# Turning the rows of eight weight-gradient blocks by DMA ahead of time, and storing them turned

## The chip, the cores and the metric

The kernel runs on one core of a Trainium2 chip. The metric is the device time of one execution in microseconds (us). A core has five engines that run side by side, each with its own queue of instructions in a fixed order: TensorE (PE: matrix products and turns of 128 x 128 blocks), VectorE (DVE), ScalarE (ACT), GpSimd (POOL) and SyncE (SP). SyncE, ScalarE and GpSimd also issue the transfers (DMAs), which run on 16 DMA engines that all queues share. An engine that waits for something holds all that is queued behind it on that engine.

## The reference

It is the backward pass of a gated mix of two branches over a sequence of L = 2048 positions with D = 448 features; all arrays are bf16. Cut to what matters:

```python
# branch A (S4): y = conv(u, K) + u * Dskip, K from A, B, C (D x 256), by FFT of 2L
# branch B: h = x @ w1 + b1; r = max(h, 0); out = (r * r) @ w2 + b2     F = 1792
g = sigmoid((u * gate_w).sum(-1, keepdims=True))
out = g * a(u) + (1 - g) * b(x)
_out, _vjp = jax.vjp(_f, u, A_re, A_im, B_re, B_im, C_re, C_im, log_dt, Dskip, w1, b1, w2, b2, gate_w)
_grads = _vjp(grad_out)            # the mix and 14 gradients are returned
```

The input x of branch B is the same array as u. With dB = (1 - g) * grad_out, the gradient of w2 (F x D) is (r * r)^T @ dB, and that of w1 (D x F) is u^T @ dh, with dh = 2 r * (dB @ w2^T). The change concerns the first of these.

## The kernel before, in words

L is cut into 16 tiles of 128 positions, F into FT = 14 blocks of 128 rows, D into 14 chunks of 32 channels for the S4 branch (NCH = 14, line 30).

The stages, in the order of the code:

- Lines 445 to 619: first transforms of u and of the gated gradient, load and turn of inputs (0 to about 230 us).
- Lines 991 to 1032, the **S4 chunks**, with c from 0 to 14: powers are built on VectorE (`build_x`, `build_y`), their tables are turned and multiplied on TensorE (`back_z`, `back_p`, `kgen`). Every chunk turns four groups g of Y: three of them by a DMA that SyncE issues (`load_yt`, line 912), the fourth (and all four of the first and the last chunk) on TensorE (`turn_yt`). The last chunk is 13, so the last DMA turn is that of chunk 12.
- Lines 597 to 619 and 1056 to 1063, `hidden`: r in four blocks of 512 positions. It is stored as rows of F in the DRAM array `rT_d` (F x L) in pieces of 256 KB; the last piece is stored at 447.6 us.
- Lines 1064 to 1083: w1 and w2 are turned on TensorE (L1071, L1082). The result of the second is the tile `w2Tv` (tag U16), and the tile `hv` (tag D16) then takes the place of w2. Both leave 1024 columns free, 7168 to 8192, which two of the seven slots of the ring `rr` use (line 1086).
- Lines 1100 to 1128 and 1152, `row_block`: dh in four blocks of 512 positions, and its product with w1 (`project`). The pieces of r come back from `rT_d` by ScalarE's queue into the ring `rr`, `NR - 3` steps ahead (L1096); VectorE multiplies (L1122) and GpSimd stores the rows of dh in `dhT_d` (L1123).
- Lines 1130 to 1155: the S4 kernel `k_d` is loaded again in another order (`X<-k_d`, L1139 and L1142, on SyncE) and transformed (L231); the transform's parts are stored and loaded again.
- Lines 1347 to 1361: the **gradient of w2**, `grad_w2(j)` for 14 blocks, then the first two of w1, with the products of the spectra (`product`) and the gradients of A, B, C (`param_grads`) woven in.
- Lines 1374 to 1460: the outputs, the remaining parameter gradients and the remaining 12 blocks of the gradient of w1.

For one block of w2 `gradrows` (line 1173) loads 128 rows of `rT_d` (512 KB) by GpSimd's queue into one of two raw buffers (L1185), turns them on TensorE in two times eight blocks of 128 x 128 into PSUM (L1190), squares them on ScalarE on the way from PSUM into one of two buffers `hn` (L1191), and multiplies them with the 16 tiles of dB (L1196, 16 products of 128 x 448). ScalarE copies the result (L1201) and GpSimd stores it (L1202). The gradient of w1 goes the same way with `dhT_d`; from block JL = 5 on, half of its rows are turned by a DMA of SyncE from DRAM (L1180).

The order on each engine isn't that of the code: a planner with costs and due times of its own orders the queues when the program is built, from what each instruction depends on; instructions earlier in the code have precedence. Work of later stages so fills gaps of earlier ones: in the trace the products of `hidden`, `project` and `row_block` stand between those of the S4 chunks. `tc.issue_after(x)` places instructions behind x on x's engine; it adds no wait. Waits are set where data or memory is needed: a tile whose memory another tile takes over is released by its last reader.

Of the kernel before, what the change touches and what calls it, by code (L numbers as in the profile page):

```python
# [12 lines left out]
ACT = mybir.ActivationFunctionType  # L13
# [6 lines left out]
P = 128  # L20
L, D, N, F = 2048, 448, 256, 1792
LT = L // P
FT = F // P
# [6 lines left out]
NCH = D // CC  # L30
# [308 lines left out]
def kernel(ctx, tc, A_u, A_A_re, A_A_im, A_B_re, A_B_im, A_C_re, A_C_im, A_log_dt, A_Dskip,  # L339
# [3 lines left out]
    nc = tc.nc  # L343
    V, S, G_, T_ = nc.vector, nc.scalar, nc.gpsimd, nc.tensor
# [5 lines left out]
    def dscr(name, n, dt=bf16):  # L350
        return nc.dram_tensor(name, (n,), dt, kind="Internal")
# [12 lines left out]
    rT_d = dscr("rT_d", F * L)  # L364
    dhT_d = dscr("dhT_d", F * L)
    br_d = dscr("br_d", L * 2 * D)

    const = ctx.enter_context(tc.tile_pool(name="const", bufs=1))
    pool = ctx.enter_context(tc.tile_pool(name="mem", bufs=1))
    psum = ctx.enter_context(tc.tile_pool(name="psum", bufs=1, space=PSUM))  # L370
    K = Ker(tc, pool, psum)
# [46 lines left out]
    SB = K.t("S25", [P, 12800])  # L418
# [137 lines left out]
    th, s, q_ = Lr_, dsa[:, 0:2 * D], dsa[:, 2 * D:4 * D]  # L556
# [208 lines left out]
    Ys = [YA[:], KB[:, 6144:14336].rearrange("p (w t b) -> p w t b", t=2, b=64)]  # L765
# [7 lines left out]
    Fv = K.t("F17", [P, 8704])  # L773
# [13 lines left out]
    P2 = K.t("M8", [P, 4096])  # L787
# [34 lines left out]
    def load_rx(c):  # L822
        rx_[c] = K.t("recx", [P, 1024])
        (G_ if c == 1 else nc.sync).dma_start(rx_[c][:], bass.AP(tensor=rec_d, offset=c * P * RS, ap=[[RS, P], [1, 1024]]))
# [87 lines left out]
    def load_yt(c, g):  # L912
        nonlocal yi
        YT = (YTr[yi % 4] if yi % 4 < 3 else P2[:, 2048:4096]).rearrange("p (h i n) -> p h i n", h=2, i=CW)
        yi += 1
        nc.sync.dma_start_transpose(out=YT.rearrange("p h i n -> p (h i) n"), in_=Ys[c % 2][:, 16 * g:16 * g + 16].rearrange("p w t b -> p (w t b)"))
        return YT

    def dk_chunk(c):
# [62 lines left out]
                        G_.dma_start(bass.AP(tensor=(t_d if s else s_d), offset=o_, ap=[[512, 32 * cnt // (1 + s)], [1, 256]]), src)  # L982
        return lastp

    XTs, YTs = {}, {}
    load_rx(0)
    load_ry(0)
    expand_x(0)
# [2 lines left out]
    for c in range(NCH + 1):  # L991
# [15 lines left out]
        for half in range(2):  # L1007
            if c < NCH:
                ay = build_y(c, half, ax if half == 0 else ap or ay)
                if half == 1:  # L1010
                    k_out(c, kgen(c))
                for g in (2 * half, 2 * half + 1):
                    YTs[c].append(turn_yt(c, g, ("S", "N3")) if c == 0 else turn_yt(c, g) if g == 3 or c == NCH - 1 else load_yt(c, g))
                if c + 1 < NCH:
                    if half == 0:
                        lry = load_ry(c + 1)
                        lry1 = lry if c == 0 else lry1
                        expand_x(c + 1)
                        if c == 0:
                            expand_y(1, 0, 4)  # L1020
                    elif c == 0:
                        expand_y(1, 4, 5)
                    else:
                        expand_y(c + 1)
                if half == 0:
                    dk_chunk(c)
            ap = None
            if c > 0:
                ap = back_p(c - 1, XTs[c - 1][half], (z01, z23)[half], (2 * half, 2 * half + 1), ay if c < NCH else None)
# [43 lines left out]
    w2Tv = K.t("U16", [P, 8192])  # L1073
# [9 lines left out]
        S.copy(w2Tw[:, jp], ps[:])  # L1083
    hv = K.t("D16", [P, 8192])
    hblk = hv[:, 0:7168].rearrange("p (j l) -> p j l", j=FT)
    rr = [P2[:, 0:1024], P2[:, 1024:2048], Fv[:, 2048:3072], Fv[:, 3072:4096], SB[:, 8320:9344], w2Tv[:, 7168:8192], hv[:, 7168:8192]]
    NR = len(rr)
    dblk = SB[:, 6272:8320].rearrange("p (a l) -> p a l", a=DT)

# [4 lines left out]
    def load_r(i):  # L1094
        r_ = rr[i % NR].rearrange("p (k l) -> p k l", k=2)
        nc.scalar.dma_start(r_, bass.AP(tensor=rT_d, offset=2 * (i % (FT // 2)) * P * L + 512 * (i // (FT // 2)), ap=[[L, P], [P * L, 2], [1, 512]]))  # L1096
        return r_
    rq = [load_r(i) for i in range(NR - 3)]

    def row_block(lb, banks):  # L1100
        nonlocal ni
# [31 lines left out]
    for (p0, p1) in ((64, 128), (32, 64), (16, 32), (0, 16)):  # L1133
        offs = vp[p0] - LT * p0
        assert all((vp[p] - LT * p == offs).all() for p in range(p0, p1))
        j = 0
# [36 lines left out]
    def gradrows(w, j, nb):  # L1173

        nonlocal hi, ni
        late = w == 1 and j >= JL
        if late:
            raw_, hh = rl[hi % 2], hl[hi % 3]
            with tc.issue_after(lasths.ins):
                nc.sync.dma_start_transpose(out=hh[:, 8:16], in_=bass.AP(tensor=dhT_d, offset=j * P * L + 1024, ap=[[L, P], [1, 1024]]))  # L1180
        else:
            raw_, hh = hr[:, hi % 2], hn[:, hi % 2]
        hi += 1
        nl = L // 2 if late else L
        K.last_raw = G_.dma_start(raw_, bass.AP(tensor=(rT_d if w == 0 else dhT_d), offset=j * P * L, ap=[[L, P], [1, nl]]))  # L1185
        for th in range(1 if late else 2):
            ps = K.ps(nb[ni % len(nb)], [P, 8, P], bf16)
            ni += 1
            for tt in range(8):
                T_.transpose(ps[:, tt, :], raw_[:, (8 * th + tt) * P:(8 * th + tt + 1) * P], ident[:])  # L1190
            S.activation(hh[:, 8 * th:8 * th + 8, :], ps[:], ACT.Square if w == 0 else ACT.Copy)  # L1191
        ps = K.ps(nb[ni % len(nb)], [P, 512])
        ni += 1
        width = D if w == 0 else D + 1
        for t in range(LT):
            lastm = T_.matmul(ps[:, 0:width], lhsT=hh[:, t, :], rhs=(DB2[:, t, :] if w == 0 else U[:, t, 0:D + 1]), start=(t == 0), stop=(t == LT - 1))  # L1196
        return ps, lastm

    def grad_w2(j):
        ps, lastm = gradrows(0, j, NB)  # L1200
        S.copy(dw2s[:, j % 2], ps[:, 0:D])  # L1201
        G_.dma_start(out_12[j * P:(j + 1) * P, :], dw2s[:, j % 2])  # L1202
        return lastm

    def grad_w1(j, nb):
        nonlocal ni
        ps, _ = gradrows(1, j, nb)
        S.copy(dw1r[:, 0:D + 1], ps[:, 0:D + 1])
        S.copy(db1[:, j:j + 1], dw1r[:, D:D + 1])
        ps = K.ps(nb[ni % len(nb)], [P, DT, P], bf16)  # L1210
        ni += 1
        for dt in range(DT):
            z = DSZ[dt]
            T_.transpose(ps[0:z, dt, :], dw1r[:, dt * P:dt * P + z], ident[:])

        j0, nj = (j - j % 2, 2) if j < JS else (JS + (j - JS) // 4 * 4, 4)
        f0, f1, dws = P * j0, P * (j - j0), (dw1a if j < JS else dw1b)
        S.copy(dws[:, 0:3, f1:f1 + P], ps[:, 0:3])
        S.copy(dws[0:64, 3, f1:f1 + P], ps[0:64, 3])
        if j == j0 + nj - 1:  # L1220
            G_.dma_start(bass.AP(tensor=out_10.tensor, offset=out_10.offset + f0, ap=[[F, P], [P * F, 3], [1, P * nj]]), dws[:, 0:3, 0:P * nj])
            G_.dma_start(bass.AP(tensor=out_10.tensor, offset=out_10.offset + 384 * F + f0, ap=[[F, 64], [1, P * nj]]), dws[0:64, 3, 0:P * nj])
# [151 lines left out]
    for q in range(4):  # L1374
# [7 lines left out]
        for x in range(2):  # L1382
            pp = K.pair()
            for hp in range(2):
                t = 2 * q + x + 8 * hp
# [32 lines left out]
    for q in range(4):  # L1418
# [5 lines left out]
        for x in range(2):  # L1424
            ps = K.pair()
            l0l = 2 * q + x
            for hp in range(2):
                t = l0l + 8 * hp
# [62 lines left out]
```

## Time and profile before

Median 921.62 us of three runs, 915.82 to 931.09. The profiled execution has a span of 918.7 us and a mean granted clock of TensorE of 0.846.

| engine | busy us | share of the span |
|---|---|---|
| TensorE, products | 719.5 | 78% |
| VectorE | 657.1 | 72% |
| ScalarE | 591.4 | 64% |
| GpSimd | 201.5 | 22% |
| DMA, hardware queue q1 (SyncE) | 118198 packets, 83.32 MB | 36.7% of 16 engines |
| DMA, software queue q0 (GpSimd) | 21504 packets, 67.46 MB | 22.1% of 16 engines |

| what | from, to (us) |
|---|---|
| S4 chunks' DMA turns, chunk 9 | 475.7 to 483.8 |
| chunk 10 | 519.5 to 529.6 |
| chunk 11 | 551.1 to 559.8 |
| chunk 12 (the last) | 582.1 to 594.8 |
| X<-k_d loads issued | 630.8 to 643.4 |
| third transform's first products (L231) | 649.6 to 662.0 |
| last row block (L1110) | 650.2 to 674.7 |
| DMA engines over 0.95 busy, TensorE mostly idle | 685 to 700 |
| gradient of w2: first turns, last product | 697.8 to 808.0 |
| gradient of w1: first turns, last product | 807.9 to 908.5 |

How to read it: the averages hide that the bound changes. VectorE is nearly full in the S4 chunks, the DMA engines are from 650 to 700 us, TensorE and VectorE in turn after it. A line of the timeline has the start, the length from first start to last end, the engine, the line of the code, the operation, the tiles by their tags (U, D, S, ... are the first letters of the pool's tags; ps with a letter is a bank of PSUM) and the count; in brackets the idle time before it and what ended it. The products' lengths overlap, since the array is pipelined: eight turns that follow each other every 0.056 us show 0.61 us.

### The profile page before, as it was taken

The page shows a single profiled execution, that of the slowest core. Times are in us where ns is not written, and L with a number is a line of the kernel's source. Part 1 is how long each engine was busy: PE and PEld are TensorE (multiplying, and loading weights), DVE is VectorE, ACT ScalarE, POOL GpSimd, SP SyncE. Part 2 cuts the span into 40 slices and gives each one's busy share as a digit, 9 for nine tenths or more (in the row PEclk, how much of TensorE's full clock was granted, in tenths as well). Part 3 has the DMA queues.
Part 4 walks back from the last instruction along what each step waited for, and adds up shares of the span by engine and source line. Part 5 has one row for each costly group of instructions (what it writes and reads, how often), then busy time and mean ns, then how long its engine had stood idle before and what let it go on. Part 6 is the DMA issues. An engine that isn't in the chain of part 4 may idle for free. (4 is left out here: it accounts for less than half of the span.)

```text
span 918.7 us, 18982 instructions
## 1 busy us (share of the span) xinstructions
PE 719.5 (78%) x7633; PEld 346.0 (38%) x7633; DVE 657.1 (72%) x1146; ACT 591.4 (64%) x939; POOL 201.5 (22%) x349
## 2 busy tenths in 40 slices
PE   1776755647988988798789887898886888988895
PEld 0332222225344443453356253344332334543352
DVE  4585867697399999979995799993424898859200
ACT  2797768716987868868676777375533765654543
POOL 2241010012202112021122031123231313354220
PEclk9977566667959798899975899899996999998998
DMA  8697675896526665357573567827999999799761
GB/s 229 191 315 254 245 291 218 322 311 188 144 58 123 149 142 115 88 127 155 124 153 79 110 210 164 185 79 202 279 388 293 334 276 350 216 256 279 193 166 52
DMA packets 167295, 184.97 MB, mean 201 GB/s; under 512 B 95187, under 2 KB 144248, under 8 KB 166408
## 3 DMA queue, kind: packets, MB, share of 16 engines
q1 hardware_dynamic: 118198, 83.32, 36.7%
q0 software_dynamic: 21504, 67.46, 22.1%
q10 hardware_dynamic: 27506, 33.00, 11.2%
q8 instruction: 59, 0.97, 0.5%
q14 instruction: 28, 0.23, 0.1%
HBM read 89.60 MB, written 73.13 MB: 177 GB/s over the span
## 5 line engine op out<-in xcount | busy, mean ns | idle before, releaser
L959 DVE TENSOR_TENSOR P<-R 128x2048 bf16<-128x2048 bf16 x42 | 49.6, 1218 | 33.0 <-ACT R L943 22.1
L943 ACT CAST R<-psF 128x1024 bf16<-128x1024 f32 x56 | 57.5, 1027 | 15.5 <-PE psF L939 15.5
L1196 PEld LDWEIGHTS <-S 128*128 128x128 bf16 x448 | 41.9, 100 | 51.9 <-issue 10.0
L1047 PE MATMUL psN<-D,S 128*128 128x448 bf16 x208 | 55.0, 400 | 4.7 <-ACT S L615 4.7
L1196 PE MATMUL psF<-U,S 128*128 128x448 bf16 x224 | 49.8, 369 | 2.8 <-ACT S L1191 2.6
L608 PE MATMUL psN<-S,U 128*128 128x512 bf16 x132 | 41.6, 434 | 8.3 <-ACT F L613 4.7
L939 PE MATMUL psF<-R,S 64*32 64x256 bf16 (+1 forms) x1344 | 38.5, 302 | 11.5 <-DMA R<-Y 7.0
L1110 PE MATMUL psN<-S,U 128*128 128x512 bf16 x126 | 37.8, 420 | 6.9 <-ACT D L1115 6.9
L209 DVE CAST K<-psN 128x448 bf16<-128x448 f32 x36 | 21.7, 619 | 28.9 <-PE psN L259 26.8
L799 DVE TENSOR_TENSOR X<-X,F 128x512 bf16<-128x512 bf16 (+1 forms) x70 | 37.5, 535 | 5.2 <-ACT F L833 3.3
L1123 POOL DMA_DIRECT2D dhT_d<-D x28 | 20.2, 721 | 92.3 <-DVE D L1122 91.7
L810 DVE TENSOR_TENSOR K<-K,F 128x2048 bf16<-128x2048 bf16 (+3 forms) x42 | 36.3, 865 | 5.0 <-ACT F L838 3.5
L810 DVE TENSOR_TENSOR Y<-Y,F 128x2048 bf16<-128x2048 bf16 (+3 forms) x42 | 36.3, 865 | 1.6
L800 DVE TENSOR_TENSOR F<-X,F 128x512 bf16<-128x512 bf16 (+1 forms) x70 | 37.0, 528 | 0.6 <-ACT F L834 0.2
L811 DVE TENSOR_TENSOR F<-K,F 128x2048 bf16<-128x2048 bf16 (+3 forms) x42 | 35.9, 854 | 2.0 <-ACT F L840 2.0
L813 DVE TENSOR_TENSOR K<-K,F 128x2048 bf16<-128x2048 bf16 (+3 forms) x42 | 36.3, 865 | 1.3
L813 DVE TENSOR_TENSOR Y<-Y,F 128x2048 bf16<-128x2048 bf16 (+3 forms) x42 | 36.3, 864 | 1.3
L909 ACT COPY M<-psX 128x1024 bf16<-128x1024 bf16 x26 | 26.5, 1019 | 15.3 <-PE psX L908 15.3
L939 PEld LDWEIGHTS <-S 64*16 64x16 bf16 (+1 forms) x1792 | 22.6, 91 | 36.0 <-issue 27.1
L811 DVE TENSOR_TENSOR F<-Y,F 128x2048 bf16<-128x2048 bf16 (+3 forms) x42 | 35.9, 855 | 0.1
L1047 PE MATMUL psN<-S,D 128*128 128x448 bf16 x168 | 35.7, 361 | 0.0
L803 DVE TENSOR_TENSOR X<-X,F 128x512 bf16<-128x512 bf16 (+1 forms) x70 | 32.4, 462 | 1.8
(412 smaller groups left out, 1948.1 us busy)
## 6 DMA issues: line engine op xcount, KB each, us to landing
sp<-K ACTq DMA_DIRECT2D x8, 896.0 KB, 4.2
hd<-st ACTq DMA_DIRECT2D x16, 448.0 KB, 5.4
dhT_d<-D POOLq DMA_DIRECT2D x28, 256.0 KB, 5.5
R<-sp SPq DMA_DIRECT2D x8, 896.0 KB, 22.2
S<-rT_d POOLq DMA_DIRECT2D x14, 512.0 KB, 7.0
R<-hd SPq DMA_DIRECT2D x16, 448.0 KB, 7.9
rec_d<-F POOLq DMA_DIRECT2D x2, 1920.0 KB, 9.7
Y<-gd SPq DMA_DIRECT2D x4, 896.0 KB, 9.2
```

The costliest lines, as they stand in the source:

```text
L608: T_.matmul(ps[:], lhsT=w1w[:, dt, j * P:j * P + P], rhs=ub[:, dt], start=(dt == 0), stop=False, skip_group_check=True)
L799: V.tensor_tensor(out=hi4, in0=lo, in1=bcast_dims(pr, [0, (None, n), 1]), op=ALU.mult)
L800: V.tensor_tensor(out=Vv.rearrange("p (x a r) -> p x a r", x=2 * W2, r=2), in0=lo, in1=bcast_dims(pi, [0, (None, n), 1]), op=ALU.mult)
L810: V.tensor_tensor(out=hi, in0=lo, in1=bcast_dims(pr, [0, (None, n // 2), 1]), op=ALU.mult)
L811: V.tensor_tensor(out=Vv.rearrange("p (x a q) -> p x a q", x=rows, q=2), in0=lo, in1=bcast_dims(pi, [0, (None, n // 2), 1]), op=ALU.mult)
L813: return V.tensor_tensor(out=T4[:, :, :, n:2 * n], in0=T4[:, :, :, n:2 * n], in1=V4, op=ALU.add)
L939: T_.matmul(psz[32 * ii:32 * ii + m, t, 256 * s:256 * s + 256], lhsT=DKc[64 * t:64 * t + 64, s, g, 2 * ii:2 * ii + 1 + par].rearrange("p i ...
L943: S.copy(zb[:, :, :, gg].rearrange("p s t n -> p t s n"), psz[:].rearrange("p t (s n) -> p t s n", s=2))
L959: lastp = V.tensor_tensor(out=pr.rearrange("p s t g n -> p s t (g n)"), in0=zv, in1=(xb if r == 0 else rev_dim(xb, 2)), op=ALU.mult)
L1047: lastm = T_.matmul(ps[:, 0:D], lhsT=hblk[j][:, P * tt:P * tt + P], rhs=ws[:, j, :], start=(w == 1 and j == 0), stop=(j == FT - 1))
L1110: T_.matmul(ps[:], lhsT=w2Tw[:, jp, dt, j % 2], rhs=dblk[:, dt], start=(dt == 0), stop=False, skip_group_check=True)
L1196: lastm = T_.matmul(ps[:, 0:width], lhsT=hh[:, t, :], rhs=(DB2[:, t, :] if w == 0 else U[:, t, 0:D + 1]), start=(t == 0), stop=(t == LT - 1))
```

## The change

The rows of r for the last eight blocks of w2's gradient (j from JN = 6 to 13) are no longer turned on TensorE in `gradrows`. Earlier, between the last S4 chunks and after them, SyncE turns them by DMA from `rT_d` into SBUF, 1024 positions (256 KB) at a time, and GpSimd stores what was turned in a new DRAM array `rN_d`. In `gradrows` such a block is then loaded from `rN_d` already turned (still 512 KB, still on GpSimd's queue), and ScalarE squares it from SBUF into `hn`. The turns and their pass through PSUM are left out for these blocks; blocks 0 to 5 and the gradient of w1 stay as they were.

The 16 DMA turns share two slots of 1024 columns, the free ends of `w2Tv` and `hv`, one for each half; turn k + 2 can't start before the store of turn k has read the slot. The ring `rr` gives these two slots up and shrinks from seven to five, so that a piece of r is loaded two steps ahead and not four. `yt_ins[c]` keeps the last DMA turn of chunk c; the turns 0 and 1 are placed behind that of chunk 9, 2 and 3 behind that of chunk 10, 4 and 5 behind that of chunk 11, and the other ten behind that of chunk 12. What it is for: to take turns from TensorE in the stage of w2's gradient.

```diff
+    rN_d = dscr("rN_d", 8 * P * L)
...
-        nc.sync.dma_start_transpose(out=YT.rearrange("p h i n -> p (h i) n"), in_=Ys[c % 2][:, 16 * g:16 * g + 16].rearrange("p w t b -> p (w t b)"))
+        yt_ins[c] = nc.sync.dma_start_transpose(out=YT.rearrange("p h i n -> p (h i) n"), in_=Ys[c % 2][:, 16 * g:16 * g + 16].rearrange("p w t b -> p (w t b)"))
...
-    rr = [P2[:, 0:1024], P2[:, 1024:2048], Fv[:, 2048:3072], Fv[:, 3072:4096], SB[:, 8320:9344], w2Tv[:, 7168:8192], hv[:, 7168:8192]]
+    rr = [P2[:, 0:1024], P2[:, 1024:2048], Fv[:, 2048:3072], Fv[:, 3072:4096], SB[:, 8320:9344]]
...
     rq = [load_r(i) for i in range(NR - 3)]
+    JN = FT - 8
+    slots = [w2Tv[:, 7168:8192], hv[:, 7168:8192]]
+    for k in range(16):
+        j, h = JN + k // 2, k % 2
+        with tc.issue_after(yt_ins[min(9 + k // 2, NCH - 2)].ins):
+            nc.sync.dma_start_transpose(out=slots[h].rearrange("p (t f) -> p t f", f=P), in_=bass.AP(tensor=rT_d, offset=j * P * L + 1024 * h, ap=[[L, P], [1, 1024]]))
+        G_.dma_start(bass.AP(tensor=rN_d, offset=(j - JN) * P * L + 1024 * h, ap=[[L, P], [1, 1024]]), slots[h])
...
-        K.last_raw = G_.dma_start(raw_, bass.AP(tensor=(rT_d if w == 0 else dhT_d), offset=j * P * L, ap=[[L, P], [1, nl]]))
-        for th in range(1 if late else 2):
+        turned = w == 0 and j >= JN
+        K.last_raw = G_.dma_start(raw_, bass.AP(tensor=rN_d, offset=(j - JN) * P * L, ap=[[L, P], [1, L]]) if turned else
+                     bass.AP(tensor=(rT_d if w == 0 else dhT_d), offset=j * P * L, ap=[[L, P], [1, nl]]))
+        if turned:
+            for th in range(2):
+                S.activation(hh[:, 8 * th:8 * th + 8, :].rearrange("p t f -> p (t f)"), raw_[:, 1024 * th:1024 * th + 1024], ACT.Square)
+        for th in range(0 if turned else 1 if late else 2):
```

More of the change, by code (lines that the diff above doesn't have):

```diff
@@ L983, in back_p @@
         return lastp
-    XTs, YTs = {}, {}
+    XTs, YTs, yt_ins = {}, {}, {}
     load_rx(0)
```

## The prediction

> **What bounds the kernel now.** I read the windows by stage first, then the timeline of TensorE in the stage the change touches, then the chain that ended last, then the queue of SyncE. The windows below cut the gradient of w2 for blocks 6 to 13 at its block boundaries (770 to 809 us). Columns: us, then busy us (and instructions) of each engine, granted clock, DMA share, GB/s.
>
> ```profile
> core 0: us, PE busy (x) PEld busy (x) DVE busy (x) ACT busy (x) POOL busy (x), PEclk, DMA share, GB/s
> 779.60:784.40 4.80, 4.56 (x37) 2.55 (x37) 4.73 (x9) 3.24 (x6) 1.63 (x3) 1.00 1.08 236
> 789.30:794.00 4.70, 4.51 (x37) 2.57 (x35) 4.67 (x6) 3.18 (x6) 1.50 (x3) 1.00 0.71 221
> 798.90:804.00 5.10, 5.10 (x39) 2.76 (x38) 1.09 (x4) 3.07 (x5) 1.47 (x4) 1.00 0.81 259
> ...
> sum 39.00, PE 37.22 PEld 20.93 DVE 31.98 ACT 23.32 POOL 14.19; mean PE 4.65 PEld 2.62 DVE 4.00 ACT 2.91 POOL 1.77
> ```
>
> TensorE is busy 37.22 of 39.00 us at full clock; VectorE is full until 800 us and then waits. One block in TensorE's timeline (start, us):
>
> ```profile
> 783.34 0.61 PE L1190 MATMUL psX<-ident,S 128*128 128x128 bf16 x8
> 783.79 0.61 PE L1190 MATMUL psS<-ident,S 128*128 128x128 bf16 x8
> 784.33 0.55 PE L314 MATMUL psN<-P,cb_MI 64*128 64x448 bf16 x3
> 785.13 3.20 PE L1196 MATMUL psF<-U,S 128*128 128x448 bf16 x16 [0.25 <-ACT S L1191]
> ```
>
> The two groups of eight turns take the array 783.34 to 784.33 less the start of the next group, 0.45 us each; then 0.55 us of other work, then a wait of 0.25 us for the square, then 3.05 us of the 16 products (the next turns start at 788.31). From the product of block 6 (770.69) to that of the first w1 block (809.73) are 39.04 us for 8 blocks: **4.88 us a block**. The chain leaves this stage by memory that the last product sets free:
>
> ```profile
> 804.99 3.04 PE psF L1196 x16
> 808.85 0.54 POOL U L1410
> ...
> 810.96 6.71 DMA U<-in_A_C_re_dram
> ```
>
> The U tile (gradient rows) is released by the last product, the A, B, C rows are loaded into it, VectorE starts its third parameter group at 815.48 and then runs without a gap to 858. So a block that ends sooner is worth its time at the end, as long as VectorE's own work (full to 800.05 us) doesn't stand in front.
>
> The place where the added work goes is SyncE's queue:
>
> ```profile
> 582.12 12.66 SPq L916 DMA_TRANSPOSE R<-Y  x3
> 630.81 0.32 SPq L1142 DMA_DIRECT2D X<-k_d  x1
> 631.33 12.10 SPq L1139 DMA_DIRECT2D X<-k_d  x10
> ```
>
> Between 594.8 and 630.8 SyncE only waits for k_d. The X loads behind that wait feed the third transform's products, which start at 649.60 with no wait; the last load is issued by 643.4 and lands 4 to 5 us later, so they have some 1.5 us of slack.
>
> **What the Trainium skill says.** "DMA: Bandwidth & Descriptors", section "Anatomy of one DMA", puts some 2 us of fixed cost on a DMA, mostly the receipt of the last write, and says that a wait happens on the issuing sequencer ahead of dispatch. The trace agrees: nothing here lands under 2 us, and SyncE sits in semaphore waits. "Advanced Engine Details and Errata", section "X-Bar Transpose (TRN2)", calls turning DMAs "as fast as regular DMAs". The trace agrees on latency only: 4.2 us median for the nine turned 256 KB loads of the end, as for the plain ones beside them. On occupancy it does not. From 876 to 900 us SyncE's queue moved 1.57 MB in 33.1% of 16 engines, 5.1 us per MB, GpSimd's 2.23 MB in 28.7%, 3.1 us per MB. The measurement decides.
>
> ```profile
> S<-dhT_d POOLq DMA_DIRECT2D x9, 256.0 KB, 4.2
> S<-dhT_d SPq DMA_TRANSPOSE x9, 4.2
> dhT_d<-D POOLq DMA_DIRECT2D x28, 256.0 KB, 5.5
> rT_d<-M POOLq DMA_DIRECT2D x8, 256.0 KB, 3.8
> ```
>
> **Removed.** 8 blocks x 16 turns leave TensorE: 8 x 2 x 0.45 = 7.2 us. The wait for the square before the product goes too (1.05 us for block 6, about 0.2 for five others, none in two): 2.1 us. Sum **9.3 us at most**, a period of 3.7 us. ScalarE keeps two squares of 1024 columns a block; the SBUF source costs the same (L615, SBUF to SBUF, 1.05 to 1.08 us; L1191 from PSUM 1.02). At 3.1 us of 4.88 it fits into 3.7.
>
> **What takes over.** A raw buffer was free when its turns were done; now it is free when its second square is done. Two buffers: the loads of this stage landed in
>
> ```profile
> DMA to landing us min/median/max: 4.0/5.6/8.1
> ```
>
> plus two squares at 0.92 us, 1.84, plus GpSimd's queue, where the load stands behind the store of the block before (it waited 16.1 us in 7 times there, beside PE; I allow 1 us). 5.6 + 1.84 + 1.0 = 8.4 us for two blocks, 4.2 a block: 0.66 us saved, x 8 = **5.3 us**. With landings of 4.0 it is 3.4, so the 3.7 of TensorE holds and 9.3 are saved; with 8.1 it is 5.5, no saving. I take 5.3.
>
> **Added, early.** Turns 0 to 5 follow the last S4 turns of chunks 9, 10, 11. Slot 0 lies in the tile that L1071 frees at 484.6, slot 1 in the one that L1082 frees at 504.5. If turn 1 stood ahead of the recx load of 493.25, that load would land at 504.5 + 1.2 + 0.3 + 3.2 = 509.2 instead of before the expansion at 506.2: 3.0 us on ScalarE, for which VectorE already waits 5.77 us there. On ScalarE the last L1083 copy (505.33) stands just ahead of that expansion, so the planner had the load issued before L1082 was done; I take 0, and keep 3.0. Turns 2 to 5 hold the next recx loads by two issues of 1.24 us; these are issued some 8 us ahead of their expansion (559.9 against 568): 0.
>
> **Added, late.** Ten turns follow the last S4 turn of chunk 12, ending at 594.8. Each slot's cycle is a turn (4.2), a store on GpSimd (0.71 to issue, 3.8 to 5.5 to land, I take 4.5): 9.4 us per pair. Turns 14 and 15 wait for four cycles: 594.8 + 37.6 = 632.4, and take 2.5 us to issue: 634.9. If the k_d loads stand behind all ten they start 4.1 us late, less 1.5 of slack: 2.6 us; ahead of the last pair, 0. Taken: **1.5 us**. Low end of the cycle, 3.4 + 0.7 + 3.0 = 7.1: nothing. High end: a store queued on GpSimd behind a dhT_d store, which waited up to 12.2 us for VectorE.
>
> DMA engines: ten turns x 0.262 MB x 5.1 = 13.3 us and ten stores x 0.262 x 3.1 = 8.1 us, 21.4 in all. The 5 us windows from 595 to 635 have shares of 0.61, 0.35, 0.07, 0.30, 0.25, 0.65, 0.66, 0.58, which leaves 22.6 us free: it just fits, hidden beside the last chunks' matmuls. What runs over 640 meets a share of 0.84 to 1.0 and would cost its own time.
>
> **Edits at nothing.** The ring of r shrinks from 7 to 5 slots. In the last row block step 5's load then waits for step 0's product (664.7) and lands by 669.4 to 672, ahead of its use at 674.3: hidden by the 1.8 us steps between. GpSimd gets 16 x 0.72 = 11.5 us more at 22% busy. DB2's load at 676 waits for slot 0's last store, which lands around 645.
>
> **Sum:** 921.6 - 5.3 + 1.5 = 917.8, **918 us**.
>
> **The rivals.**
> 1. The turns hold SyncE. Stores land late because GpSimd is held by dhT_d stores, so pairs take 12 us: turn 15 is issued at 594.8 + 48 + 2.5 = 645.3, the X loads start 14.5 late, 13 past the slack: 921.6 + 13 - 5.3 = 929. For it: the 12.2 us wait and one queue in order. Against: only four dhT_d stores stand from 605 to 622, and the planner may let the loads overtake. 25%.
> 2. The same, with every store behind such a wait (17 us a pair): 594.8 + 68 + 2.5 = 665, 34.5 late, 33 past the slack, 921.6 + 33 - 5.3 = 949: slower than before. 10%.
> 3. TensorE's full 9.3 us come, nothing is late: 912. For it: landings of 4.0 to 4.7 after 785 us, where DMA share falls to 0.27. Against: VectorE, full to 800. 15%.
> 4. The ring of two raw buffers becomes the bound at 8.1 us landings, no gain: 921.6 + 1.5 = 923. For it: 7.2, 7.8 and 8.1 us for three of seven loads. 8%.
>
> **How the numbers follow.** The forecast has 42%. Its parts alone (landings 4.0 to 8.1, cost 0 to 3) span 912 to 924. Rival 1 reaches from 920 to 935. A range of **909 to 933** leaves out rival 2, part of rival 1's tail and a few per cent below. The three times of before lie from 915.8 to 931.1, so some of the range is that. Faster than 903.2 would need twice 9.3 us: 4%. Slower than 940.1 is rival 2 and a remainder: 11%. Within: 85%.
>
> **What would show it.** Right: a period of about 4.2 us in blocks 6 to 13, L1410 loads some 4 us sooner against the start of the stage, X<-k_d issued by 635, SyncE's turns done before. Wrong: X<-k_d issued after 640 (rivals 1, 2); waits of the square for the raw load of over 2 us a block (rival 4); waits of S4 products for turned tiles grown past today's 12.6 us; or VectorE as the releaser of the products, so that the shorter blocks buy nothing.

## The result, and the profile after

The changed kernel takes **946.63 us** (median of six runs, 942.30 to 955.99); the kernel before took 924.08 us beside it (six runs, 915.82 to 935.40). The ratio is **1.029, 95% interval 1.021 to 1.037**: slower. Medians are over all executions of a kernel, while a ratio and its interval compare only the fast ones of either kernel (within 1.5% of its fastest), so the two can differ. In the later comparisons the median of before was 924.7 to 926.7 us, so 921.6 was a somewhat kind start, and its profiled execution of 918.7 us kinder still. A second profile of the kernel before is used below where that matters (span 914.1 us, called "before, again").

The same stage as in the prediction, the gradient of w2 from the product of block 6 to the first of w1, now lies at 790.5 to 827.9 us. The windows of the changed kernel by stage, three of eight blocks (columns as in the prediction):

```profile
core 0: us, PE busy (x) PEld busy (x) DVE busy (x) ACT busy (x) POOL busy (x), PEclk, DMA share, GB/s
...
799.10:808.80 9.70, 3.20 (x16) 1.48 (x16) 9.60 (x17) 2.89 (x6) 2.17 (x4) 0.88 1.01 282
...
814.00:817.00 3.00, 3.00 (x18) 1.57 (x16) 2.83 (x8) 2.44 (x3) 1.19 (x3) 1.00 0.62 187
...
sum 37.50, PE 28.47 PEld 13.86 DVE 30.05 ACT 19.41 POOL 14.41; mean PE 3.56 PEld 1.73 DVE 3.76 ACT 2.43 POOL 1.80
```

TensorE's busy time in the stage fell from 37.22 to 28.47 us, but the stage only from 39.0 to 37.5. Some 5.7 of these 8.75 us are not saved but moved: 33 products of the inverse transforms (L314, L331, L333) stood between the turns of these blocks and took 6.28 us; in the changed kernel 3 are left (0.55 us), and nearly all of the others run after the stage. The undisturbed block at 814 runs in 3.0 us; the one at 799 takes 9.7, with the DMA engines full. TensorE's timeline says what it waits for (start and length in us; in brackets the idle time before and what ended it):

```profile
794.21 3.20 PE L1209 MATMUL psS<-U,S 128*128 128x448 bf16 x16 [0.54 <-ACT S L1198]
799.19 3.20 PE L1209 MATMUL psF<-U,S 128*128 128x448 bf16 x16 [1.78 <-ACT S L1198]
808.90 5.32 PE L1209 MATMUL psX<-U,S 128*128 128x448 bf16 x16 [6.51 <-ACT S L1198]
814.05 3.19 PE L1209 MATMUL psS<-U,S 128*128 128x448 bf16 x16
```

The squares (L1198) in turn wait for the raw rows. The first line below is from that line's own view (who kept ScalarE idle, us and times), the second from the page's DMA issues (512 KB each, median 6.3 us to landing):

```profile
  DMA S<-rN_d: 14.7, 5
...
S<-rN_d POOLq DMA_DIRECT2D x8, 512.0 KB, 6.3
```

So the gradient gave little. The loss is earlier. SyncE's queue in the changed kernel:

```profile
582.46 11.61 SPq L917 DMA_TRANSPOSE R<-Y  x3
594.16 3.05 SPq L1105 DMA_TRANSPOSE U<-rT_d  x1
...
631.66 1.28 SPq L1105 DMA_TRANSPOSE D<-rT_d  x1
642.95 0.33 SPq L1150 DMA_DIRECT2D X<-k_d  x1
643.38 12.75 SPq L1147 DMA_DIRECT2D X<-k_d  x10
```

The issue of the last turn ends at 632.9 us, 2.0 us *sooner* than I had worked out (634.9). Yet the first load of k_d comes at 642.95, against 630.81 before. SyncE did not hold it: between 633 and 643 it waits for k_d itself. GpSimd's queue has the reason:

```profile
629.32 0.54 POOL L1106 DMA_DIRECT2D rN_d<-D  x1 [5.65 <-DMA D<-rT_d]
...
638.44 0.56 POOL L1106 DMA_DIRECT2D rN_d<-D  x1 [5.38 <-DMA D<-rT_d]
639.00 2.42 POOL L885 DMA_DIRECT2D k_d<-R  x4
```

Four of the last chunk's k_d stores stand behind the store of turn 15. Their data was there at 623; they are issued from 639.0 on. In the kernel before the same four were issued as soon as their data was there:

```profile
624.62 2.43 POOL L884 DMA_DIRECT2D k_d<-R  x4
```

ScalarE issues the other four. Its queue before, and then in the changed kernel:

```profile
625.35 2.65 ACTq L884 DMA_DIRECT2D k_d<-R  x4
628.04 1.01 ACT L909 COPY R<-psX 128x1024 bf16<-128x1024 bf16 x1 [4.44 <-PE psX L908]
```

```profile
623.66 8.25 ACTq L885 DMA_DIRECT2D k_d<-R  x4
631.95 1.01 ACT L910 COPY R<-psX 128x1024 bf16<-128x1024 bf16 x1 [8.79 <-issue]
```

The same four issues took 2.65 us before and 8.25 us beside the turns, and the copies behind them, which the last S4 chunk's products wait for, came 3.9 us later. So there are two suspects for k_d, the **order on GpSimd** and the **slow issue on ScalarE**, and a third, the sheer traffic.

To compare kernels whose executions drift, I count from one event in each: the start of the last product of the S4 kernel (`kgen`, 623.1 us before, 622.6 after).

| us after the last k product | before | before, again | changed |
|---|---|---|---|
| first load X<-k_d | 7.7 | 7.4 | 20.3 |
| first turns of w2's gradient | 74.7 | 75.0 | 88.0 |
| from there to the first product of w1's gradient | 111.9 | 119.7 | 117.3 |
| from there to the end of the span | 109.0 | 109.2 | 112.6 |

13 us are lost at k_d and carried unchanged to the gradient. The third row needs its second column: in blocks 0 to 5 TensorE met a wait of 7 us that the first profile of before did not have. It ends in the evacuations of L208. Before, again:

```profile
754.34 0.53 PE L331 MATMUL psN<-R,negI 128*128 128x448 bf16 x1 [7.04 <-ACT st L208]
```

In the changed kernel it is 7.98 us at 778. It comes and goes without the change, so it isn't counted to it.

### The profile page after: what moved, and what is told of

Read it like the earlier page. It is cut to its first block, busy times and chain, and to the rows that moved or that the text cites. A ratio compares the mean times of both kernels' runs of the same rounds, so it can differ in the third digit from the quotient of the medians.

```text
span 940.5 us, 18791 instructions
## 1 busy us (share of the span) xinstructions
PE 717.7 (76%) x7505; PEld 340.0 (36%) x7505; DVE 656.6 (70%) x1146; ACT 591.7 (63%) x939; POOL 210.6 (22%) x365
## 3 DMA queue, kind: packets, MB, share of 16 engines
q1 hardware_dynamic: 135094, 87.51, 39.6%
## 5 line engine op out<-in xcount | busy, mean ns | idle before, releaser
L800 DVE TENSOR_TENSOR X<-X,F 128x512 bf16<-128x512 bf16 (+1 forms) x70 | 37.4, 535 | 5.2 <-ACT F L834 3.3
L1048 PE MATMUL psN<-S,D 128*128 128x448 bf16 x168 | 38.1, 379 | 2.0 <-DVE D L1130 2.0
L940 PEld LDWEIGHTS <-S 64*16 64x16 bf16 (+1 forms) x1792 | 22.9, 91 | 39.6 <-issue 30.5
L314 PE MATMUL psN<-P,cb_MI 64*128 64x448 bf16 x128 | 29.0, 402 | 9.5 <-ACT st L208 8.2
L1209 PE MATMUL psF<-U,S 128*128 128x448 bf16 x128 | 32.7, 396 | 2.6 <-ACT S L1198 1.8
```

Of the source, the lines that this page charges most:

```text
L800: V.tensor_tensor(out=hi4, in0=lo, in1=bcast_dims(pr, [0, (None, n), 1]), op=ALU.mult)
L940: T_.matmul(psz[32 * ii:32 * ii + m, t, 256 * s:256 * s + 256], lhsT=DKc[64 * t:64 * t + 64, s, g, 2 * ii:2 * ii + 1 + par].rearrange("p i ...
L1048: lastm = T_.matmul(ps[:, 0:D], lhsT=hblk[j][:, P * tt:P * tt + P], rhs=ws[:, j, :], start=(w == 1 and j == 0), stop=(j == FT - 1))
```

## The experiments

Times are medians; "before" is the kernel before in the same comparison, and a ratio has its 95% interval. The edits are against the changed kernel unless "before" is said.

### 1. Which part: the turns, or their use?

Two halves. First, all turns and stores made and the ring cut, but the gradient as it was:

```diff
-        turned = w == 0 and j >= JN
+        turned = False
```

> The changed kernel with all 16 DMA turns and their stores, and the ring of five slots, but the last eight blocks of w2's gradient are loaded from rT_d and turned on TensorE as before. Theory K (the last chunk's k_d stores stand behind the store of the last turn on GpSimd, so the third transform starts 12 us late and that carries to the end): before + 10 to 13 us, a ratio of 1.011 to 1.014 to before, X<-k_d issued at about 643. Rival G (the loss is made in the gradient of w2, where ScalarE waits 14.7 us for turned rows; the 12 us are absorbed while the DMA engines are full): before + 0 to 3 us, ratio 1.000 to 1.003.

Measured: 947.69 us (before 926.26), ratio 1.022 (1.013 to 1.032). X<-k_d 15.2 us after the last k product, first turns of w2's gradient 85.1 after it. So nearly all of the loss is here, and it is larger than I had expected.

Second, the kernel before with the gradient's edit alone, on rows that were not turned:

```diff
# against before
+        turned = w == 0 and j >= JN
+        K.last_raw = G_.dma_start(raw_, bass.AP(tensor=rT_d, offset=j * P * L, ...) if turned else ...
+        if turned:
+            for th in range(2):
+                S.activation(hh[...], raw_[:, 1024 * th:1024 * th + 1024], ACT.Square)
```

> No turns and no stores of them, seven slots in the ring of r as before; the last eight blocks are loaded from rT_d as they are and squared straight from SBUF, without any turn (so these blocks of w2's gradient are of rows that were not turned: the work of turning is left out). Theory K: before - 1 to - 6 us, ratio 0.993 to 0.999. Rival G: before + 6 to 10 us, ratio 1.007 to 1.011, with ScalarE waiting over 10 us for the loads.

Measured: 922.78 us (before 926.26), ratio 0.997 (0.994 to 1.000). So the use is worth some 3.5 us by the medians and 2.4 by the ratio, whose interval just reaches 1: a gain, but less than the 5.3 that I took. Together the halves give 17.9 of the 22.6 us; the first half's interval is wide enough for the rest. The squares waited as they do in the changed kernel; from the view of their line:

```profile
  DMA S<-rT_d: 14.2, 4
```

### 2. How many turns does it take?

Three blocks: the six early turns alone, with the short ring.

```diff
-    JN = FT - 8
+    JN = FT - 3
-    for k in range(16):
+    for k in range(6):
```

> The changed kernel for the last three blocks only: the six early turns (behind chunks 9, 10 and 11), none behind chunk 12. Theory K: nothing stands before the k_d stores; before + 0 to - 2 us (three blocks at 0.66), ratio 0.998 to 1.000. Rival G: three eighths of its loss, before + 2 to + 4, ratio 1.002 to 1.004.

Then five, six and seven blocks, by the same two numbers (`FT - 5` and `range(10)`, `FT - 6` and `range(12)`, `FT - 7` and `range(14)`).

> The changed kernel with five turned blocks in place of eight: ten turns, of which four are late and over by about 612, ahead of the k_d stores at 622. Theory Q: X<-k_d at 624 to 632 as in the kernel before, ratio 0.994 to 1.003. Rival C (each late turn costs its share of the traffic, 4 of 10 late turns): ratio 1.008 to 1.013, and X<-k_d 4 to 5 us late.

> The changed kernel with six turned blocks: twelve turns, six of them late, the last issued at about 615 and its store landed by about 621, just ahead of the k_d stores. Theory T (the cost is a cliff: it starts when turns and their stores reach into the k_d stores and loads, from 622 on): X<-k_d 7 to 10 us after the last k product, as before, ratio 0.998 to 1.005. Rival L (each late turn costs its share, 20 us over the last six): ratio 1.006 to 1.010.

> The same with seven turned blocks: fourteen turns, the last issued at about 623, its store at about 628 ahead of GpSimd's four k_d stores. Theory T: half of the cliff, X<-k_d 12 to 16 us after the last k product (before: 8, changed kernel: 20), first turns of the second weights' gradient 79 to 84 us after it (before: 75, changed kernel: 88), ratio 1.006 to 1.016. Rival (only the last pair of turns hurts, since it alone holds SyncE): ratio 0.998 to 1.005.

| turned blocks | turns after chunk 12 | against before, us | ratio | X<-k_d, us after last k product | first turns of w2, us after it |
|---|---|---|---|---|---|
| 3 | 0 | +0.4 | 1.003 (1.000 to 1.006) | 7.8 | 77.6 |
| 5 | 4 | +1.2 | 1.002 (0.998 to 1.006) | 6.6 | 74.1 |
| 6 | 6 | +3.2 | 1.005 (1.001 to 1.009) | 8.8 | 78.2 |
| 7 | 8 | +17.9 | 1.018 (1.011 to 1.024) | 17.1 | 87.5 |
| 8 | 10 | +22.6 | 1.029 (1.021 to 1.037) | 20.3 | 88.0 |

It is a step, not a slope. Theory T holds in kind and was too mild for seven blocks, where nearly all of the delay is there already (the profile with seven blocks is of the slowest of four executions, 954.9 us). SyncE's queue with six and with seven blocks shows the step:

```profile
613.51 1.28 SPq L1105 DMA_TRANSPOSE D<-rT_d  x1
627.90 0.33 SPq L1150 DMA_DIRECT2D X<-k_d  x1
```

```profile
627.41 1.23 SPq L1105 DMA_TRANSPOSE U<-rT_d  x1
635.29 1.23 SPq L1105 DMA_TRANSPOSE D<-rT_d  x1
647.01 0.33 SPq L1150 DMA_DIRECT2D X<-k_d  x1
```

With six, the last turn is issued 5.6 us ahead of the last k product (619.1) and its store issued at 618.0. With seven, the last one stands 5.4 us behind that product (629.9), and ScalarE's four k_d issues take 9.30 us there instead of 4.74. Even 4.74 is more than the 2.65 of before, though with six blocks every turn had landed by 618.0, ahead of these issues; so a turn under way isn't all that slows them. The early six turns show no cost beyond the noise (the interval reaches 1.006), as I had said.

### 3. Which queue, then?

If GpSimd's order was to blame, ScalarE could issue all eight k_d stores of the last chunk:

```diff
-                    (nc.scalar if jt and c > 9 else G_).dma_start(bass.AP(tensor=k_d, ...
+                    (nc.scalar if c > 9 else G_).dma_start(bass.AP(tensor=k_d, ...
```

> The changed kernel with one edit: the four k_d stores of the last chunk that GpSimd issues behind the last turn's store are issued by ScalarE, right behind the copy that they store. The order of TensorE, VectorE and SyncE stays as it is in the changed kernel. Theory K: X<-k_d is issued at 633 instead of 643 (then held only by SyncE's own last turn), and the time falls by 8 to 10 us against the changed kernel: 936 to 938, ratio to before 1.013 to 1.015. Rival G: the loads are earlier but the time stays within 2 us of the changed kernel, ratio 1.027 to 1.031.

Measured: 941.26 us (before 926.26), ratio 1.021 (1.013 to 1.029); X<-k_d 16.7 us after the last k product, and w2's gradient 87.2 after it. A miss: the wait only changed its queue. ScalarE's queue in this kernel:

```profile
622.84 15.98 ACTq L885 DMA_DIRECT2D k_d<-R  x8
638.86 1.01 ACT L910 COPY R<-psX 128x1024 bf16<-128x1024 bf16 x1 [16.53 <-DMA k_d<-R]
```

Eight issues at 2.0 us each, where before one took 0.66 us, and ScalarE's own work stood behind them for 16.5 us.

The other way round: all eight on GpSimd, and the stores of turns 12 to 15 placed behind them.

```diff
-                    (nc.scalar if jt and c > 9 else G_).dma_start(bass.AP(tensor=k_d, ...
+                    kd_ins[0] = G_.dma_start(bass.AP(tensor=k_d, ...
...
+        with tc.issue_after(kd_ins[0].ins) if k >= 12 else nullcontext():
             G_.dma_start(bass.AP(tensor=rN_d, ...), slots[h])
```

> The changed kernel, with all eight k_d stores of the last chunk on GpSimd and the stores of the last four turns put behind them, so that neither ScalarE issues k_d stores nor a store of a turn that is still to come stands ahead of them. Theory Q (the order in GpSimd's queue and ScalarE's slow issue made k_d late): first X<-k_d load at 632 to 637 against 643, third transform at 650 to 655, ratio 1.000 to 1.010, time 926 to 935. Rival C (the traffic itself makes k_d and all behind it late): X<-k_d after 639, ratio 1.015 to 1.03.

Measured: 942.09 us (before 926.71), ratio 1.016 (1.013 to 1.020). X<-k_d began 10.9 us after the last k product, so both suspects were cured for the k_d stores. And yet w2's gradient began 88.4 us after it, no sooner than in the changed kernel. SyncE's queue shows the next place:

```profile
628.40 0.33 SPq L1153 DMA_DIRECT2D X<-k_d  x1
630.46 1.41 SPq L1107 DMA_TRANSPOSE U<-rT_d  x1
632.96 3.18 SPq L1107 DMA_TRANSPOSE D<-rT_d  x1
636.24 11.17 SPq L1150 DMA_DIRECT2D X<-k_d  x10
```

The planner put the first load ahead of turns 14 and 15, and the other ten behind them, where they waited for the two slots: 18.7 to 29.9 us after the last k product against 8.2 to 20.3 before. On GpSimd the stores of these two turns now held the stores of the S4 sums instead of those of k_d:

```profile
638.17 0.55 POOL L1109 DMA_DIRECT2D rN_d<-U  x1 [6.09 <-DMA U<-rT_d]
642.96 0.54 POOL L1109 DMA_DIRECT2D rN_d<-D  x1 [4.24 <-DMA D<-rT_d]
```

So neither theory had it whole. Q was right on k_d's first load, C on the ratio; the time came back by another queue, because a turn that is not over by then holds something wherever it is put.

### 4. Is it the turning, or the bytes?

The same loads, slots and queues, without the turn:

```diff
-            nc.sync.dma_start_transpose(out=slots[h].rearrange("p (t f) -> p t f", f=P), in_=bass.AP(tensor=rT_d, ...))
+            nc.sync.dma_start(slots[h], bass.AP(tensor=rT_d, ...))
```

> The changed kernel with plain loads of the same rows in place of the turns (the second weights' gradient of blocks 6 to 13 is then summed over the wrong axis). Same bytes, same slots, same queues. Theory A (turning is what slows ScalarE's issue of the k_d stores): these four issues take 0.7 us each again instead of some 2, the rest of the delay stays as far as the slot cycle (about 7 us a pair in place of 8) allows: X<-k_d at 632 to 637, ratio 1.005 to 1.015. Theory B (any traffic of that size in that stretch does it): ScalarE's four issues still take 6 to 9 us, X<-k_d after 638, ratio 1.015 to 1.03.

Measured: 935.95 us (before 926.71), ratio 1.012 (1.009 to 1.016). X<-k_d 10.9 us after the last k product; ScalarE's four k_d issues took 4.19 us, between the 2.65 of before and the 8.25 of the changed kernel. The last plain load was issued at 619.1, ahead of the last k product (619.5). So more than half of the loss (9.2 us are left of 22.6) goes with the turning, and not with the bytes or the queues: the ten late loads were issued in 31.2 us as plain ones (587.9 to 619.1) and in 37.5 as turns (594.2 to 631.7). Since they were over sooner, this run doesn't part what a turn slows by itself from what it holds by ending late. On ScalarE's issues neither theory was right (A had 2.8 us, B 6 to 9). The rest stays with the same stores and loads in the same queues; X<-k_d is 3 us late here, and the rest of it comes after that load. w2's gradient began 83.7 us after the last k product.

### 5. The ring of r

The kernel before with five slots instead of seven.

> The kernel before with the ring of r tiles cut from seven slots to five, as the change does. Expected by every theory: ratio 0.998 to 1.003. Against it: the loads of r of the last row block, which start later, fall among the k_d loads and ScalarE waits for them: ratio 1.003 to 1.01.

Measured: 927.21 us (before 924.70), ratio 1.005 (1.002 to 1.007), so about 2.5 us by the medians and 4.4 by the ratio: more than every theory had. X<-k_d and w2's gradient lie where they lay (6.7 and 75.0 us after the last k product), so these 2.5 us are not at the place that I named against it; where they are wasn't found.

### 6. Where the gain of the gradient went

One more raw buffer for the squared blocks in the kernel of part 1 that uses unturned rows (a part of memory that is free until w1's gradient):

```diff
# against before with the gradient's edit alone
             raw_, hh = hr[:, hi % 2], hn[:, hi % 2]
+            if w == 0 and j >= JN:
+                raw_ = (hr[:, 0], hr[:, 1], SB[:, 9600:11648])[(j - JN) % 3]
```

> The kernel before with blocks 6 to 13 of the second weights' gradient squared straight from the unturned rows (so their sums are over the wrong axis), as one of the runs before, and now with three raw buffers in place of two for these blocks. Theory J (the ring of two raw buffers took most of the gain): waits of ScalarE for the raw rows fall from some 15 us to below 4, ratio 0.991 to 0.995 against 0.997 with two. Rival V (the stage is held by something else, such as VectorE's own work, so that shorter blocks buy nothing): ratio 0.996 to 1.000, same as with two.

> Once more, with more rounds: the kernel before with blocks 6 to 13 squared straight from the unturned rows (sums over the wrong axis) and three raw buffers. If the 7 to 8 us by which its second weights' gradient was shorter reach the end: ratio 0.988 to 0.994. If the tail gives them back (its tail was 113.4 us from the first product of the first weights' gradient to the end, against 109.0 before): ratio 0.995 to 1.000.

Measured: 917.12 us (before 926.71), ratio 0.985 (0.977 to 0.993), from four runs; again with more runs 917.18 us (before 925.17), ratio 0.988 (0.985 to 0.992). And the third buffer alone, with the turns left on TensorE:

```diff
# against before
             raw_, hh = hr[:, hi % 2], hn[:, hi % 2]
+            if w == 0 and j >= 6:
+                raw_ = (hr[:, 0], hr[:, 1], SB[:, 9600:11648])[(j - 6) % 3]
```

> The kernel before with one addition alone: blocks 6 to 13 of the second weights' gradient take their raw rows from three buffers in turn in place of two, and are still turned on TensorE. Theory J (the third buffer helps only where squares hold a raw buffer; with turns on TensorE the period is TensorE's 4.5 us and the loads are ahead): ratio 0.997 to 1.002. Rival (the raw loads already held the kernel before, so the third buffer alone brings what the run with three buffers and no turns brought): ratio 0.983 to 0.992.

> Once more, with more rounds: the kernel before with three raw buffers for blocks 6 to 13, turned on TensorE as before. If the third buffer lifts waits of its own: ratio 0.987 to 0.995. If the first look was a kind draw: 0.997 to 1.002.

Measured: 921.68 us (before 924.70), ratio 0.987 (0.979 to 0.996), from four runs; again with more runs 925.91 us (before 925.17), ratio 0.998 (0.994 to 1.002). The first four runs were a kind draw; alone, the buffer brings nothing. So the squares hold the raw buffers: without turns, two buffers give 3.5 us and three give 8.0 by the medians (2.4 and 10.8 by the ratios), close to the 9.3 that I had as the most. The wait of the squares with three buffers, from the view of their line:

```profile
  DMA S<-rT_d: 5.6, 3
```

From the product of block 6 to the first of w1 this kernel took 31.6 us (780.1 to 811.7), where before took 39.0, the two-buffer kernel 37.8 (775.3 to 813.1) and the changed kernel 37.4.

### 7. Two tries for a better version

Five turned blocks, with the third raw buffer for them:

> Five turned blocks (ten turns by DMA, over by about 612) and a third raw buffer for them. Theory: nothing is late at the k_d stores, and five blocks run at TensorE's 3.05 us of products: five eighths of what the run with three buffers and no turns brought, ratio 0.988 to 0.994, X<-k_d at 624 to 632. Rival (the loads of the turned rows or VectorE's work hold these blocks in spite of the third buffer): ratio 0.998 to 1.004.

Measured: 924.37 us (before 924.70), ratio 1.005 (0.999 to 1.011). X<-k_d 7.1 us after the last k product, so nothing was late there; but no gain at the end. And all sixteen turns drawn forward, with the third buffer:

```diff
-        with tc.issue_after(yt_ins[min(9 + k // 2, NCH - 2)].ins):
+        with tc.issue_after(yt_ins[min(9 + k // 4, NCH - 2)].ins):
```

> The changed kernel with the sixteen turns drawn forward to four after each of chunks 9 to 12 in place of two (so that four are late, as with five blocks), and a third raw buffer for the turned blocks. Theory: no turn reaches the k_d stores, X<-k_d 7 to 10 us after the last k product; the stage gains what the run with three raw buffers and no turns gained (8 us) less what the shorter ring of r costs (2 us): ratio 0.990 to 0.996. Rival: turns between the chunks hold the recx and recy loads on SyncE while they wait for their slots (a store of 5 us and a turn of 4 each), S4 becomes longer by 2 to 6 us for each of three chunks: ratio 1.000 to 1.015.

Measured: 931.17 us (before 925.20), ratio 1.007 (1.004 to 1.011). The last turn is well ahead of the first load of k_d:

```profile
614.08 1.29 SPq L1105 DMA_TRANSPOSE D<-rT_d  x1
636.59 0.33 SPq L1150 DMA_DIRECT2D X<-k_d  x1
```

X<-k_d came 6.5 us after the last k product (630.1) and w2's gradient 74.8: with the same sixteen turns and stores, only placed sooner, **the 13 us are gone**. This settles that place and not number makes the delay. The rest of what I expected failed: the kernel is 6 us slower, not faster. Its gradient of w2 took 114.5 us (before, again: 119.7), and from there to the end 115.9 us instead of 109. The ratio is the one that the rival had (1.000 to 1.015), and the trace shows longer S4 chunks, as the rival had them, though not that the held loads are their cause: from the copy of chunk 8's k product (L879; L878 in the kernel before), which comes ahead of the first turn, to that of the last one the S4 chunks took 171.5 us, against 153.7 to 163.0 in the eight profiles of kernels without turns. (The profile is of a 937.6 us execution, slower than the median.) No version that does the whole work beat the kernel before.

### 8. The kernel before, again

> The kernel before once more, to see which of its stages vary from one execution to the next: the profile shown in the prediction is of 918.7 us. Expected: first turns of the second weights' gradient at 693 to 700 us, and the stage from there to the first product of the first weights' gradient at 112 to 120 us, where the profile shown has 111.9 us.

Measured: 915.89 us. The first turns of w2's gradient were at 685.2, sooner than I said; the stage to the first product of w1's gradient took 119.7 us. This is the column "before, again" above.

## Why the prediction was wrong

**The bound of the stage, right in kind.** I said that the ring of two raw buffers takes over when the squares hold them, with 4.2 us a block. Blocks 6 to 13 went from 4.88 to 4.7 us a block in the changed kernel (37.44 / 8); undisturbed ones ran at 3.0. The term was mis-sized: I priced a landing at 5.6 us, and in the changed kernel the median was 6.3, with 9.5 once: by the same sum, (6.3 + 1.84 + 1.0) / 2 = 4.6 us a block. Measured without the turns, it is 3.5 us with two buffers in place of 5.3. Part 6 shows the mechanism by taking it away: 8.0 with three. Rival 4, "the ring becomes the bound, no gain", was near in the changed kernel.

**Work that moved, at nothing.** I took it that all the rest of a block's work on TensorE stays where it is. In the changed kernel, 30 of the 33 products of the inverse transforms left the blocks. After the first product of w1's gradient TensorE has 185 products of these lines, 28.9 us, where before has 156, 23.4 us. So part of what the stage saved comes back in the tail, which is 3.4 us longer.

**Early turns, right.** I took 0 for turns 0 to 5 with 3.0 kept; six early turns with the ring and three blocks' gain are +0.4 us (ratio 1.000 to 1.006).

**"Added, late ... Taken: 1.5 us", the step that failed.** Measured: 13 us at X<-k_d, which stand undiminished at the start of w2's gradient. The working of the turns' times was good (the last one's issue ended at 632.9, I had 634.9), and it answered the wrong question. I asked how long the turns hold SyncE, and what holds the *turns' stores* on GpSimd. I did not ask what the turns' stores hold: the four k_d stores of the last chunk stand behind them on GpSimd, and these end the wait of every X load. I had read "between 594.8 and 630.8 SyncE only waits for k_d" as free time for SyncE, and taken k_d's own time as fixed. The Trainium skill's "DMA: Bandwidth & Descriptors", section "Anatomy of one DMA", which I quoted for a wait on the issuing sequencer ahead of dispatch, describes GpSimd's own path; the trace shows such a wait with the 5.38 us ahead of 638.44. (My reading that nothing lands under the 2 us of that section was not exact: two small stores of the kernel before landed in 1.6 and 1.7 us.)

**"GpSimd gets 11.5 us more at 22% busy", at nothing: wrong for the same reason.** The issues do take 0.54 us each. But 13 of the stores waited on GpSimd for a turn to land. A queue's busy share says nothing of what its waits hold up.

**ScalarE's issue, not foreseen.** The issue of a k_d store took 0.66 us before and 2.0 us beside late turns (part 3). I had no term for that. In the changed kernel it isn't what ends the wait for k_d: ScalarE's last issue was over at 631.9, GpSimd's at 641.4.

**DMA traffic "just fits": half right.** I had read the 22.6 us of free DMA time as room for 21.4 us of turns and stores. Plain loads of the same bytes cost 13 us less than turns in the whole kernel (9.2 against 22.6, each against its own runs of before). On the same queue of SyncE the sixteen turns took some 17 us more of the 16 DMA engines than the plain loads (39.6% of 940.5 us against 37.9% of 937.3). The Trainium skill's "Advanced Engine Details and Errata", section "X-Bar Transpose (TRN2)", calls them as fast; the occupancy that I had measured (5.1 against 3.1 us per MB) was the better guide, as far as it went.

**The ring at nothing: wrong by about 2.5 us** by the medians (ratio 1.005, 1.002 to 1.007, which is 4.4).

**The rivals.** Rivals 1 and 2 had the right place (X<-k_d after 640, the sign that I had set for them) and the right size between them, 929 and 949, but the wrong mechanism: the stores of the turns were not held by dhT_d stores so that SyncE was late; they were themselves in front, waiting for their own turns. Both had the sign, and rival 2 came nearest to the size. Rival 3, everything free, was the farthest off.

**U sooner.** I said that the loads of U come 4 us sooner against the start of the stage. Counted from the product of block 6 they began after 36.1 us (790.5 to 826.6), against 37.6 in the first profile of before (770.7 to 808.3) and 37.5 in the other: 1.5 us sooner, the gain of the stage.

**What stays open.** 13 us at k_d, 2.5 of the ring and 3.4 of the tail, less the 2 to 3 us of the gradient, make some 16 of the 22.6 us.

The tail, from the first product of w1's gradient to the end, took 108.5 to 109.5 us in the five profiles of kernels with neither DMA turns nor squared blocks, and 111 to 117 in the others. The moved products can explain most of it: with 156 of them in the tail, and its granted clock at 0.94, it took the shorter time, and with 166 to 185, at 0.94 to 0.95, 111.1 to 114.1. The kernel of part 1 with its turns unused doesn't fit: 156 products and 116.3 us, at a clock of 0.90. So a lower clock may add its share; that wasn't tested by itself.

It may also be that the S4 chunks get slower. Up to chunk 8's k product, ahead of all turns, eight profiles without turns have 458.8 us on average and eleven with turns, or the plain loads in their place, 457.3. From there to the last k product they have 158.9 (153.7 to 163.0) and 165.4 (161.1 to 171.5). The changed kernel's own profile, with 161.2 against the 159.4 and 161.1 of before, shows next to nothing of it. The clock over the last four chunks was 0.90 to 0.94 without turns and 0.88 to 0.93 with them, so whether the traffic or the clock makes the difference isn't shown.

The granted clock was lower in the whole, too: 0.828 on average for the changed kernel, 0.838 for the kernel before, and among 193 runs of the latter 0.01 less went with 4.8 us more (correlation -0.67). Whether the clock is a cause of the rest or goes along with it, no run tells.

## What to carry to other kernels

Work that is put "into a gap" of an engine has to be followed through every queue that it enters: ask not only what the new instructions wait for, but what stands behind them on the queue that issues their stores, and who waits for that. A helper transfer must be over, store included, before the next transfer on the critical path is ready; count its cycles back from that moment (here, in the places that the change gave them, twelve turns did fit and fourteen did not; drawn forward, sixteen did). And when a buffer's release moves from an early reader to a late one, the number of buffers has to grow with it, or the gain stays in the wait. Time taken from one engine in one stage can also be work that the planner moved: count the same lines in the stages behind it.

## What the runs showed of the hardware

- The issue of a small-row store (k_d<-R) by ScalarE is not a fixed cost: 0.66 us before, 1.0 beside plain loads on SyncE's queue, 2.0 beside turning ones (2.65, 4.19 and 8.25 us for four; 15.98 for eight), and 1.2 just after the last turn with six blocks (4.74 for four). ScalarE's computing waits for as long.
- Making plain loads of the sixteen turns took away more than half of the loss (9.2 us left of 22.6), though bytes and slots were the same; the plain loads were also over sooner.
- A store that waits on GpSimd's queue for its data holds later stores whose data is there: four k_d stores, ready at 623, were issued from 639.0 on.
- One program on one core varied from 908.8 to 939.6 us over 193 runs, more than most edits here moved it, and TensorE's wait of 7 to 8 us in the third transform's inverse (L208) was there in some executions of one program and not in others. Two four-run results (0.985 and 0.987) looked alike; with more runs one stayed (0.988) and one went (0.998).
